# The last row of w4 as a stationary operand, and a result stored from 128 partitions

## Chip, core and metric

One NeuronCore of a Trainium2 chip runs the kernel. The metric is the device time of one execution in microseconds (us); of several runs the median is taken. A separate execution is taken by the hardware profiler. It gives the span from the first to the last instruction, the busy time of each engine and each packet that the 16 DMA engines move.

The engines are PE (TensorE, the matrix unit; the loading of its stationary operand is listed apart as PEld), DVE (VectorE), ACT (ScalarE), POOL (GpSimd) and SP (SyncE, which here only issues transfers).

## The reference

One token `x` of 1024 numbers goes through an attention block over a long cache and, beside it, through a small mixer with an MLP; both results are added to `x`. The batch and the sequence length are 1.

```python
xn = layernorm(x)                              # [1, 1, 1024]
# A: 32 query heads, 4 key/value heads, 65536 cached positions, head size 128
q  = (xn @ wq).reshape(32, 128)                 # wq: [1024, 4096]
p  = softmax(q @ k.T * 128**-0.5)              # k, v: [4, 65536, 128], each for 8 query heads
A  = (p @ v).reshape(4096) @ wo                # wo: [4096, 1024]
# B, with xB = xn
h  = gelu(layernorm(xn) @ w1)                  # w1, w2: [1024, 1024]
hs = shifted(h) @ w2                           # with one position every shift brings in zeros
x1 = xn + hs
B  = x1 + gelu(layernorm(x1) @ w3) @ w4        # w3: [1024, 3584], w4: [3584, 1024]
out = x + A + B
```

All inputs and the output are bf16. Keys and values together are 134 MB and the weights 36 MB, so 170 MB are read for one output of 2 KB.

## The kernel before

**Loads.** SP issues every large load into eight slots of 16 KB per partition. A list `loads` gives their order: wq, w1, w2, w3, then keys and values of eight groups with the four parts of wo between them, and at the end wo's last part and w4. A slot is used again once its last reader is done; SP waits for that ahead of the load, and all loads behind it in the list wait too. w4 has 3584 = 28 x 128 rows, so that each partition holds 28 of them, here called rows 0 to 27. They come as one load of 16 rows (two slots), then rows 16 to 23 in four pieces of two rows, then rows 24 to 27 in pieces of 2, 1 and 1 (`w4_split`). Each piece has a semaphore of its own.

**Layout.** A vector of 1024 numbers has two layouts. In the first, partition p holds the 8 numbers 8p to 8p+7 (`xP`, `xn`, `x1`). In the second, "rows", the numbers lie on 4 partitions (0, 32, 64, 96) with 256 on each. A product of a vector and a matrix is made by `rows_mv` (L440): the vector is the stationary operand, 32 columns wide, of which one column is of use, and the matrix is the moving operand in four parts of 256 columns, one for each quarter of the array (`tile_position`). Its result is in rows, on partitions 0, 32, 64 and 96 of a PSUM bank. Where a product is needed in the first layout, `to_p` (L444) turns it with DVE's 32x32 transpose.

**The sum.** Bank `M1_ps`, columns 0 to 255, gathers in rows what w2 (L440, from `use_w2`), the four parts of wo and all 28 rows of w4 contribute. The rest of the output, x + xn, is kept in rows as `accr`: x is loaded a second time by ACT's queue into `xr_bf` on partitions 0, 32, 64 and 96 (L393, after a memset at L392), and two operations of DVE (L627, L629) normalise it with the sums of the first layer norm and add x. That load shares the semaphore `ch_x` with the load of `xP_bf` (L391), and the cast at L395, from which the first layer norm starts, waits for both.

**The end.** After row 27, DVE adds `accr` and `M1_ps` into `fin`, 128x256 in bf16 of which four partitions are of use (L678), and SP stores these four with one DMA of four pieces of 512 bytes (L679), waits for it and ends.

Each engine runs its own list of instructions in order; `_op` and `_grp` put the waits for semaphores ahead of an instruction by the buffers that it reads and writes (`b_M0`, `b_M1`, `b_fin` and so on). Bank `M0_ps` serves the small products: layer norm sums, the heads' combination and others.

Of the kernel before, what the change touches and what calls it, by code (L numbers as in the profile page):

```python
# [6 lines left out]
BF = mybir.dt.bfloat16  # L7
F32 = mybir.dt.float32
ACTF = mybir.ActivationFunctionType
ALU = mybir.AluOpType  # L10
# [64 lines left out]
def _deps(q, reads, writes):  # L75
    for b in reads:
        for s, v in b.w.items():
            q.wait((s, v))
    for b in writes:
        for s, v in b.w.items():  # L80
            q.wait((s, v))
        for s, v in b.r.items():
            q.wait((s, v))


def _done(ev, reads, writes, partial=False):
    for b in reads:
        b.add_read(ev)
    for b in writes:
        if partial:  # L90
            b.add_write(ev)
        else:
            b.set_write(ev)


def _op(q, fn, reads=(), writes=(), partial=False):
    _deps(q, reads, writes)
    ev = q.op(fn, True)
    _done(ev, reads, writes, partial)
    return ev  # L100


def _grp(q, fns, reads=(), writes=(), partial=False):
    _deps(q, reads, writes)
    ev = None
    for i, fn in enumerate(fns):
        ev = q.op(fn, i == len(fns) - 1)
    _done(ev, reads, writes, partial)
    return ev
# [8 lines left out]
def _dma(q, chan, fn, reads=(), writes=(), partial=False):  # L118
    _deps(q, reads, writes)
    chan.n += 1  # L120
    ev = q.dma(fn, chan.sem, 16 * chan.n)
    _done(ev, reads, writes, partial)
    return ev
# [10 lines left out]
def bass_parallel_sum__gqa_block_cached__mixer_s_mlp__decode_kernel(  # L134
# [14 lines left out]
    P = 128  # L149
    D = A_x.shape[2]  # L150
# [5 lines left out]
    R = D // P  # L156
# [8 lines left out]
    NT = F // P  # L165
    CL = CR // 4
    RW = D // 4
# [7 lines left out]
    with ExitStack() as es:  # L175
# [3 lines left out]
        def sb(name, shape, dt):  # L179
            return E(nc.sbuf_tensor(name, shape, dt))  # L180

        def ps(name, shape, dt):
            return E(nc.psum_tensor(name, shape, dt))

        def sem(name):
            return E(nc.semaphore(name))
# [16 lines left out]
        xP = sb("xP", [P, R], F32)  # L203
        xn = sb("xn", [P, R], F32)
# [6 lines left out]
        ln_s = sb("ln_s", [P, 8], F32)  # L211
# [20 lines left out]
        cb_m = sb("cb_m", [P, 16, R], F32)  # L232
        cb_o = sb("cb_o", [P, R], F32)
        oP_bf = sb("oP_bf", [P, HKV * R + 32], BF)
        xr_bf = sb("xr_bf", [P, RW], BF)
        accr = sb("accr", [P, RW], F32)
        g_bf = sb("g_bf", [P, R + 32], BF)
        ge_x = sb("ge_x", [P, NT], F32)
        ge_a = sb("ge_a", [P, NT], F32)
        ge_b = sb("ge_b", [P, NT], F32)  # L240
        h1g_bf = sb("h1g_bf", [P, R], BF)
        gh_bf = sb("gh_bf", [P, NT + 32], BF)
        fin = sb("fin", [P, RW], BF)

        S_all = ps("S_ps", [P, NCH * 512], F32)
        S_ps = [S_all[:, 512 * i:512 * (i + 1)] for i in range(NCH)]
# [2 lines left out]
        M0_ps = ps("M0_ps", [P, 512], F32)  # L249
        M1_ps = ps("M1_ps", [P, 512], F32)  # L250

        q_pe = _Q("pe", sem("c_pe"))
        q_dve = _Q("dve", sem("c_dve"))
        q_act = _Q("act", sem("c_act"))
        q_pool = _Q("pool", sem("c_pool"))
        q_sp = _Q("sp", None)
        ch_x = _DmaChan(sem("d_x"))
        ch_out = _DmaChan(sem("d_out"))
# [3 lines left out]
        b_ln = _B(); b_qT = _B(); b_Y = _B(); b_misc = _B(); b_ge = _B()  # L262
# [5 lines left out]
        b_Bst = _B(); b_brun = [_B(), _B()]; b_dd = _B(); b_ff = _B()  # L268
        b_p = _B(); b_pT = [_B(), _B()]; b_lcol = [_B(), _B()]; b_lsum = _B(); b_Lacc = _B(); b_O = _B()
        b_cb = _B(); b_oP = [_B() for _ in range(HKV)]  # L270
        b_xr = _B(); b_accr = _B(); b_h1 = _B(); b_gh = _B(); b_fin = _B()


        place = [0]
# [15 lines left out]
        def load(src, width=SLOT):  # L290
            i = take(1, 1)
            view = slots_sb[:, i, 0:width]
            _dma(q_sp, slots[i].chan, lambda e, view=view, src=src: e.dma_start(out=view, in_=src), writes=[slots[i].buf])
            return [(view, [slots[i].buf], i)]
# [94 lines left out]
        b_const.set_write(ev)  # L389

        _dma(q_act, ch_x, lambda e: e.dma_start(out=xP_bf[:, :], in_=A_x[0, 0, :].rearrange("(p r) -> p r", p=P)), writes=[b_xb])  # L391
        _op(q_dve, lambda e: e.memset(xr_bf[:], 0.0), writes=[b_xr])  # L392
        _dma(q_act, ch_x, lambda e: e.dma_start(out=xr_bf[0:P:32, :], in_=A_x[0, 0, :].rearrange("(j m) -> j m", j=4)), writes=[b_xr])  # L393
        b_xb.add_write((ch_x.sem, 16 * ch_x.n))
        _op(q_dve, lambda e: e.tensor_copy(xP[:], xP_bf[:]), reads=[b_xb], writes=[b_x])  # L395

        _op(q_pe, lambda e: e.matmul(M1_ps[:, 0:P], selGT_bf[:, :], selGT_bf[:, :], start=True, stop=True), reads=[b_const], writes=[b_M1])
# [36 lines left out]
        def rows_mv(nkk, parts, st_fn, b_st, b_slot, b_out, first, last, k0=0):  # L434
            fns = []
            for kk in range(k0, k0 + nkk):
                for out_fn, mv_fn in parts:
                    for j in range(4):
                        fns.append(lambda e, kk=kk, j=j, out_fn=out_fn, mv_fn=mv_fn, st=(first and kk == k0), sp=(last and kk == k0 + nkk - 1):
                                   e.matmul(out_fn(j), st_fn(kk), mv_fn(kk, j), start=st, stop=sp, tile_position=(0, 32 * j), skip_group_check=True))  # L440
            _grp(q_pe, fns, reads=b_slot + [b_st], writes=b_out, partial=not first)
# [4 lines left out]
        def gelu(width, dst_bf, b_dst):  # L446
            xs_ = ge_x[:, 0:width]; a_ = ge_a[:, 0:width]; bb_ = ge_b[:, 0:width]
            _op(q_dve, lambda e: e.tensor_copy(xs_, X32[:, 1, 0:32 * width:32]), reads=[b_X[1][0]], writes=[b_ge])
            _op(q_dve, lambda e: e.tensor_tensor(out=a_, in0=xs_, in1=xs_, op=ALU.mult), reads=[b_ge], writes=[b_ge])
            _op(q_dve, lambda e: e.tensor_scalar(out=a_, in0=a_, scalar1=0.044715, scalar2=1.0, op0=ALU.mult, op1=ALU.add), reads=[b_ge], writes=[b_ge])  # L450
            _op(q_dve, lambda e: e.tensor_tensor(out=bb_, in0=a_, in1=xs_, op=ALU.mult), reads=[b_ge], writes=[b_ge])  # L451
            _op(q_act, lambda e: e.activation(a_, bb_, ACTF.Tanh, scale=math.sqrt(2.0 / math.pi)), reads=[b_ge], writes=[b_ge])  # L452
            _op(q_dve, lambda e: e.tensor_scalar(out=a_, in0=a_, scalar1=1.0, scalar2=0.5, op0=ALU.add, op1=ALU.mult), reads=[b_ge], writes=[b_ge])
            _op(q_dve, lambda e: e.tensor_tensor(out=dst_bf, in0=a_, in1=xs_, op=ALU.mult), reads=[b_ge, b_const], writes=[b_dst])
# [23 lines left out]
        def d_parts(view, c0):  # L478
            return [(lambda t: M1_ps[32 * t:32 * t + 32, c0:c0 + RW], lambda kk, t: view[:, kk * D + t * RW:kk * D + (t + 1) * RW])]
# [14 lines left out]
        def use_w3(j, ld):  # L494
# [4 lines left out]
            if j == 3:  # L499
                to_p(S_all[:, 1024:1024 + FW].rearrange("p (c s) -> p s c", s=NT), 0, NT, [b_S[2], b_S[3]])  # L500
                gelu(NT, gh_bf[:, 0:NT], b_gh)

        def use_w4(grp, ld):
            view, parts = ld[0:2]
            for bu, k0, k in parts:
                rows_mv(k, d_parts(view, 0), lambda kk: gh_bf[:, grp * R + kk:grp * R + kk + 32], b_gh, bu, [b_M1],
                        False, grp * R + k0 + k == NT, k0)

        def use_wo(h, ld):
            view, b = ld[0:2]  # L510
# [99 lines left out]
        for g in range(NG):  # L610
# [13 lines left out]
        uses += [("v", NG - 1, a) for a in range(NA)] + [("wo", HKV - 1)] + [("w4", i) for i in range(4)]  # L624

        layer_norm(xP, b_x, xn, xn_bf, b_xn, 0)
        _op(q_dve, lambda e: e.tensor_scalar(out=accr[:], in0=xr_bf[:], scalar1=ln_s[:, 1:2], scalar2=ln_s[:, 4:5], op0=ALU.add, op1=ALU.mult),  # L627
            reads=[b_xr, b_ln], writes=[b_accr])
        _op(q_dve, lambda e: e.tensor_tensor(out=accr[:], in0=accr[:], in1=xr_bf[:], op=ALU.add), reads=[b_xr, b_accr], writes=[b_accr])  # L629
        loaders = {"wq": load_wq, "w1": lambda: load(w1_v[:, 0:SLOT]), "w2": lambda: load(w2_v[:, 0:SLOT]), "w3": load_w3, "wo": load_wo, "w4": load_w4,  # L630
                   "k": load_k, "v": load_v}
        doubles = {"wq", "w3", "k"}
# [42 lines left out]
                taken[i] -= 1  # L675
            issue()
        assert not loads and not ready
        _op(q_dve, lambda e: e.tensor_tensor(out=fin[:], in0=accr[:], in1=M1_ps[:, 0:RW], op=ALU.add), reads=[b_accr, b_M1], writes=[b_fin])  # L678
        ev_out = _dma(q_sp, ch_out, lambda e: e.dma_start(out=out[0, 0, :].rearrange("(j m) -> j m", j=4), in_=fin[0:P:32, :]), reads=[b_fin])  # L679
        q_sp.wait(ev_out)  # L680

        block.sync(lambda e: q_sp.emit(e))
# [32 lines left out]
```

## Time and profile before

| | |
|---|---|
| median of 3 runs | 406.20 us (406.18 to 406.21) |
| the profiled execution's own time | 406.29 us |
| its span, first to last instruction | 404.6 us |
| mean granted TensorE clock | 0.615 |
| busy: PE, PEld, DVE, ACT, POOL | 170.8, 75.4, 200.4, 65.2, 7.5 us |
| bytes moved, mean rate | 170.13 MB, 421 GB/s |
| the largest group of DVE: L522, transposes of keys | 147.7 us, 128 of 1211 ns |

How to read it: a group of instructions is named by line, engine and operation, the tiles that it writes and reads, and its shape; `M_ps` stands for both banks M0 and M1, and `in_B_w_dram` for w1 to w4. An arrow with a name after it tells what ended the idle time before the group. "SPq" and "ACTq" are instructions that issue transfers. A DMA's landing is the moment when its semaphore has its last count. Cut into stages, the page's rows give for each stage the busy time of PE, PEld, DVE, ACT and POOL, the granted clock, the share of time that the 16 DMA engines are busy, and GB/s.

### The profile page before, as it was taken

The page shows a single profiled execution, that of the slowest core. Times are in us where ns is not written, and L with a number is a line of the kernel's source. Part 1 is how long each engine was busy: PE and PEld are TensorE (multiplying, and loading weights), DVE is VectorE, ACT ScalarE, POOL GpSimd, SP SyncE. Part 2 cuts the span into 40 slices and gives each one's busy share as a digit, 9 for nine tenths or more (in the row PEclk, how much of TensorE's full clock was granted, in tenths as well). Part 3 has the DMA queues.
Part 4 walks back from the last instruction along what each step waited for, and adds up shares of the span by engine and source line. Part 5 has one row for each costly group of instructions (what it writes and reads, how often), then busy time and mean ns, then how long its engine had stood idle before and what let it go on. Part 6 is the DMA issues. An engine that isn't in the chain of part 4 may idle for free.

```text
span 404.6 us, 4047 instructions
## 1 busy us (share of the span) xinstructions
PE 170.8 (42%) x1651; PEld 75.4 (19%) x1651; DVE 200.4 (50%) x304; ACT 65.2 (16%) x91; POOL 7.5 (2%) x38
## 2 busy tenths in 40 slices
PE   0273231223555345435335363535252436355626
PEld 0122110102212112211121131212121122122313
DVE  0255027667667665755173737571545655740010
ACT  1000000006007105200610041106010232034000
POOL 5000000000000000000000000000000000000000
PEclk9985655555655965665556655656565657655656
DMA  8999999999999999999999999999999999999995
GB/s 357 421 415 426 452 415 444 413 437 420 462 400 431 429 447 411 441 414 444 411 450 410 437 424 441 415 427 439 423 433 434 423 434 424 420 434 420 444 405 197
DMA packets 9682, 170.13 MB, mean 421 GB/s; under 512 B 1208, under 2 KB 1216, under 8 KB 2112
## 3 DMA queue, kind: packets, MB, share of 16 engines
q1 hardware_dynamic: 9512, 169.88, 98.5%
q8 instruction: 13, 0.21, 0.2%
q14 instruction: 5, 0.04, 0.0%
q10 hardware_dynamic: 152, 0.00, 0.0%
HBM read 169.87 MB, written 0.00 MB: 420 GB/s over the span
## 4 chain that ended last, share of the span: by engine, by line
DMA 57%; DVE 21%; PE 13%; issue 6%; ACT 2%; SPq 0%; POOL 0%; ACTq 0%
DMA slots_sb<-in_A_k_cache_dram 47%; DVE X L522 17%; PE S_ps L529 8%; DMA slots_sb<-in_B_w_dram 7%; DMA xr_bf<-in_A_x_dram 3%; DVE mcol L534 3%; PE OT_ps L575 2%; PE S_ps L440 2%; ACT p_sb L553 1%; ACT pT_sb L565 1%; PE PT_ps L562 1%; PE M_ps L424 0%; PE M_ps L416 0%; PE M_ps L543 0%; SPq L317 0%
## 5 line engine op out<-in xcount | busy, mean ns | idle before, releaser
L522 DVE STREAM_TRANSPOSE X<-slots_sb 128x1024 f32<-128x1024 f32 x128 | 147.7, 1211 | 39.1 <-DMA slots_sb<-in_A_k_cache_dram 39.1
L529 PE MATMUL S_ps<-X,Yall 128*32 128x512 bf16 x512 | 59.9, 614 | 150.4 <-DVE X L522 150.4
L553 ACT ACTIVATE p_sb<-S_ps,brun 128x512 bf16<-128x512 f32 x32 | 45.2, 1412 | 195.5 <-DVE brun L545 105.2
L575 PE MATMUL OT_ps<-slots_sb,pT_sb 128*32 128x512 bf16 x512 | 55.9, 584 | 12.8 <-ACT pT_sb L565 9.6
L534 DVE TENSOR_REDUCE mcol<-S_ps 128x1 f32<-128x512 f32 x32 | 22.1, 692 | 69.2 <-PE S_ps L529 69.2
L529 PEld LDWEIGHTS S_ps<-X,Yall 128*32 128x32 bf16 x512 | 17.3, 126 | 185.8 <-DVE X L522 169.4
L575 PEld LDWEIGHTS OT_ps<-slots_sb,pT_sb 128*32 128x32 bf16 x512 | 18.5, 132 | 37.9 <-issue 32.2
L565 ACT ACTIVATE pT_sb<-PT_ps 128x1024 bf16<-128x1024 bf16 x16 | 16.4, 1023 | 55.6 <-PE PT_ps L562 55.6
L562 PE MATMUL PT_ps<-ident_bf,p_sb 128*128 128x128 bf16 x128 | 15.3, 294 | 11.8 <-ACT pT_sb L565 8.9
L440 PE MATMUL S_ps<-slots_sb,xn_bf 128*32 128x512 bf16 (+1 forms) x128 | 12.6, 567 | 10.7 <-DMA slots_sb<-in_B_w_dram 9.2
L562 PEld LDWEIGHTS PT_ps<-ident_bf,p_sb 128*128 128x128 bf16 x128 | 11.4, 133 | 20.3 <-ACT pT_sb L565 11.0
L592 DVE TENSOR_TENSOR O_acc<-O_acc,OT_ps 128x512 f32<-128x512 f32 x4 | 2.8, 688 | 16.5 <-PE OT_ps L575 16.5
L440 PE MATMUL M_ps<-slots_sb,gh_bf 128*32 128x256 bf16 x112 | 6.5, 399 | 7.7 <-DMA slots_sb<-in_B_w_dram 7.6
L444 DVE STREAM_TRANSPOSE X<-S_ps 128x512 f32<-128x512 f32 (+1 forms) x3 | 2.5, 848 | 14.2 <-PE S_ps L440 14.2
L452 ACT ACTIVATE ge_a<-ge_b 128x8 f32<-128x8 f32 (+1 forms) x2 | 0.4, 217 | 52.2 <-DVE ge_b L451 52.2
L678 DVE TENSOR_TENSOR fin<-accr,M_ps 128x256 bf16<-128x256 f32 x1 | 0.4, 421 | 16.3 <-PE M_ps L440 16.3
L553 ACT ACTIVATION_READ_ACCUMULATOR p_sb<-S_ps,brun 128x1 f32 x32 | 8.5, 264 | 0.0
L440 PE MATMUL M_ps<-slots_sb,oP_bf 128*32 128x256 bf16 x128 | 7.7, 420 | 1.4 <-DVE oP_bf L604 1.4
L597 PE MATMUL M_ps<-O_acc,selX 128*128 128x128 f32 x32 | 8.2, 439 | 0.0
L440 PEld LDWEIGHTS S_ps<-slots_sb,xn_bf 128*32 128x32 bf16 x128 | 4.3, 133 | 17.0 <-DMA slots_sb<-in_B_w_dram 9.9
L597 PEld LDWEIGHTS M_ps<-O_acc,selX 128*128 128x128 f32 x32 | 7.3, 333 | 0.0
L395 DVE CAST xP<-xP_bf 128x8 f32<-128x8 bf16 x1 | 0.2, 172 | 14.2 <-DMA xr_bf<-in_A_x_dram 14.2
(97 smaller groups left out, 70.1 us busy)
## 6 DMA issues: line engine op xcount, KB each, us to landing
slots_sb<-in_A_k_cache_dram SPq DMA_DIRECT2D x16, 4096.0 KB, 26.9
slots_sb<-in_A_v_cache_dram SPq DMA_DIRECT2D x32, 2048.0 KB, 30.7
slots_sb<-in_A_wq_dram SPq DMA_DIRECT2D x2, 4096.0 KB, 16.8
slots_sb<-in_A_wo_dram SPq DMA_DIRECT2D x4, 2048.0 KB, 27.5
slots_sb<-in_B_w_dram SPq DMA_DIRECT2D x2, 3584.0 KB, 33.5
slots_sb<-in_B_w_dram SPq DMA_DIRECT2D x2, 2048.0 KB, 28.1
slots_sb<-in_B_w_dram SPq DMA_DIRECT2D x1, 4096.0 KB, 31.9
slots_sb<-in_B_w_dram SPq DMA_DIRECT2D x5, 512.0 KB, 32.4
```

The costliest lines, as they stand in the source:

```text
L440: e.matmul(out_fn(j), st_fn(kk), mv_fn(kk, j), start=st, stop=sp, tile_position=(0, 32 * j), skip_group_check=True))
L444: _op(q_dve, lambda e: e.transpose(out=X32[:, 1, c0:c0 + 32 * n], in_=src), reads=b_src, writes=[b_X[1][0]], partial=c0 > 0)
L452: _op(q_act, lambda e: e.activation(a_, bb_, ACTF.Tanh, scale=math.sqrt(2.0 / math.pi)), reads=[b_ge], writes=[b_ge])
L522: _op(q_dve, lambda e, ix=ix: e.transpose(out=X32[:, m, 1024 * ix:1024 * (ix + 1)], in_=K32[:, 1024 * ix:1024 * (ix + 1)]), reads=b, write ...
L529: fns.append(lambda e, we=we, c_mid=c_mid, mv=mv: e.matmul(S_ps[ch][32 * c_mid:32 * c_mid + 32, :], Yall[:, h, we, :, :].rearrange("p a g ...
L534: _op(q_dve, lambda e: e.reduce_max(mcol[:, gm, ch:ch + 1], S_ps[ch][:, :], axis=AX.X), reads=[b_S[ch]], writes=[b_mcol[gm]], partial=ch > 0)
L553: _op(q_act, lambda e, ch=ch: e.activation(p_sb[:, :, :, ch], S_ps[ch][:, :].rearrange("p (c i) -> p c i", i=32), ACTF.Exp, bias=brun[:, k ...
L562: _grp(q_pe, [lambda e, i=i, c=8 * c8 + i: e.transpose(out=PT_ps[:, i * P:(i + 1) * P], in_=p_sb[:, c, :, :].rearrange("p i h -> p (i h)") ...
L565: _op(q_act, lambda e, c8=c8, m=m: e.activation(pT_sb[:, m, :, 32 * c8:32 * c8 + 32, :].rearrange("p a x g -> p x a g"), PT_ps[:, :].rearr ...
L575: fns.append(lambda e, cl=cl, q4=q4: e.matmul(OT_ps[32 * q4:32 * q4 + 32, :], pT_sb[:, m, a, 4 * cl:4 * cl + 4, :].rearrange("p x g -> p ( ...
L592: _op(q_dve, lambda e: e.tensor_tensor(out=O_acc[:, :], in0=O_acc[:, :], in1=OT_ps[:, :], op=ALU.add), reads=[b_OT], writes=[b_O])
L597: fns.append(lambda e, t=t: e.matmul(M0_ps[:, 256:384], selX[:, t, :, :].rearrange("p g x -> p (g x)"), O_acc[:, t * P:(t + 1) * P], start ...
```

## The change

The output is gathered in the first layout, on all 128 partitions. `acc` = x + xn is made there with one addition, so the second load of x, its memset and the two operations in rows go. All rows of w4 but the last still go through `rows_mv` into `M1_ps`. When row 26 is done, `turn_acc` turns the sum to 128 partitions with DVE's transpose and adds it to `acc`. Row 27 is multiplied the other way about: for each c of 0 to 7, the 128 columns c, c+8, c+16 and so on of w4's row are the stationary operand (read with a step of 8 elements, 16 bytes), one column of `gh_bf` is the moving operand, and the result is one column of `M0_ps` on 128 partitions. `fin` becomes 128x8, and the store takes 16 bytes from each of 128 partitions.

```diff
-        xr_bf = sb("xr_bf", [P, RW], BF)
-        accr = sb("accr", [P, RW], F32)
+        acc = sb("acc", [P, R], F32)
+        accT = sb("accT", [P, 32 * R], F32)
...
-        fin = sb("fin", [P, RW], BF)
+        fin = sb("fin", [P, R], BF)
...
-        _op(q_dve, lambda e: e.memset(xr_bf[:], 0.0), writes=[b_xr])
-        _dma(q_act, ch_x, lambda e: e.dma_start(out=xr_bf[0:P:32, :], in_=A_x[0, 0, :].rearrange("(j m) -> j m", j=4)), writes=[b_xr])
-        b_xb.add_write((ch_x.sem, 16 * ch_x.n))
...
+        LAST = 1
+
+        def turn_acc():
+            _op(q_dve, lambda e: e.transpose(out=accT[:, :], in_=M1_ps[:, 0:RW].rearrange("p (c r) -> p r c", r=R)), reads=[b_M1], writes=[b_accT])
+            _op(q_dve, lambda e: e.tensor_tensor(out=acc[:], in0=acc[:], in1=accT[:, 0:32 * R:32], op=ALU.add), reads=[b_accT], writes=[b_acc])
+
         def use_w4(grp, ld):
             view, parts = ld[0:2]
             for bu, k0, k in parts:
-                rows_mv(k, d_parts(view, 0), lambda kk: gh_bf[:, grp * R + kk:grp * R + kk + 32], b_gh, bu, [b_M1],
-                        False, grp * R + k0 + k == NT, k0)
+                k1 = grp * R + k0
+                if k1 < NT - LAST:
+                    rows_mv(k, d_parts(view, 0), lambda kk: gh_bf[:, grp * R + kk:grp * R + kk + 32], b_gh, bu, [b_M1], False, k1 + k == NT - LAST, k0)
+                    if k1 + k == NT - LAST:
+                        turn_acc()
+                    continue
+                _grp(q_pe, [lambda e, kk=kk, c=c, st=(k1 == NT - LAST and kk == k0 and c == 0): e.matmul(M0_ps[:, 32 + c:33 + c], view[:, kk * D + c:(kk + 1) * D:R], gh_bf[:, grp * R + kk:grp * R + kk + 1],
+                                                           start=st, stop=(grp * R + kk == NT - 1), skip_group_check=True)
+                            for kk in range(k0, k0 + k) for c in range(R)], reads=bu + [b_gh], writes=[b_M0], partial=k1 > NT - LAST)
...
-        _op(q_dve, lambda e: e.tensor_scalar(out=accr[:], in0=xr_bf[:], scalar1=ln_s[:, 1:2], scalar2=ln_s[:, 4:5], op0=ALU.add, op1=ALU.mult),
-            reads=[b_xr, b_ln], writes=[b_accr])
-        _op(q_dve, lambda e: e.tensor_tensor(out=accr[:], in0=accr[:], in1=xr_bf[:], op=ALU.add), reads=[b_xr, b_accr], writes=[b_accr])
+        _op(q_dve, lambda e: e.tensor_tensor(out=acc[:], in0=xP[:], in1=xn[:], op=ALU.add), reads=[b_x, b_xn], writes=[b_acc])
...
-        _op(q_dve, lambda e: e.tensor_tensor(out=fin[:], in0=accr[:], in1=M1_ps[:, 0:RW], op=ALU.add), reads=[b_accr, b_M1], writes=[b_fin])
-        ev_out = _dma(q_sp, ch_out, lambda e: e.dma_start(out=out[0, 0, :].rearrange("(j m) -> j m", j=4), in_=fin[0:P:32, :]), reads=[b_fin])
+        _op(q_dve, lambda e: e.tensor_tensor(out=fin[:], in0=acc[:], in1=M0_ps[:, 32:32 + R], op=ALU.add), reads=[b_acc, b_M0], writes=[b_fin])
+        ev_out = _dma(q_sp, ch_out, lambda e: e.dma_start(out=out[0, 0, :].rearrange("(p r) -> p r", p=P), in_=fin[:, :]), reads=[b_fin])
         q_sp.wait(ev_out)
```

More of the change, by code (lines that the diff above doesn't have):

```diff
@@ L270, in bass_parallel_sum__gqa_block_cached__mixer_s_mlp__decode_kernel @@
         b_cb = _B(); b_oP = [_B() for _ in range(HKV)]
-        b_xr = _B(); b_accr = _B(); b_h1 = _B(); b_gh = _B(); b_fin = _B()
+        b_acc = _B(); b_accT = _B(); b_h1 = _B(); b_gh = _B(); b_fin = _B()
         place = [0]
```

## The prediction

> **What bounds the kernel now.** I began with the page: is the end set by an engine or by the transfers?
>
> ```profile
> span 404.6 us, 4047 instructions
> ...
> DMA  8999999999999999999999999999999999999995
> ```
>
> The DMA row stands at its highest digit in every slice but the first and the last. DVE, the busiest engine, has 50% of the span. To see whether the digit 9 hides gaps I cut the span into stages:
>
> ```profile
> 20.00:40.00 20.00, 11.49 (x136) 5.85 (x128) 11.14 (x52) 0.21 (x1) 1.10 (x2) 0.70 0.98 418
> 40.00:200.00 160.00, 64.19 (x606) 25.31 (x606) 91.55 (x115) 29.98 (x43) 0.00 (x0) 0.59 1.00 429
> 200.00:380.00 180.00, 80.86 (x736) 35.21 (x740) 92.84 (x119) 33.76 (x47) 0.00 (x0) 0.59 1.01 429
> ...
> 401.70:404.60 2.90, 0.28 (x4) 0.08 (x4) 0.42 (x1) 0.00 (x0) 0.00 (x0) 0.79 0.00 1
> ```
>
> The last two columns are the DMA share and GB/s. From 2.5 to 396 us, the two stages not shown included, the share is 0.98 to 1.01: no wait between engines there lengthens the kernel, for the transfers never pause. The time is therefore the stream of 169.9 MB plus what stands after its last byte. I followed that end in the chain of waits and then in the timeline:
>
> ```profile
> 373.81 27.82 DMA slots_sb<-in_B_w_dram
> 401.64 0.04 issue
> 401.68 0.32 PE M_ps L440 x4
> 402.00 0.02 issue
> 402.03 0.42 DVE fin L678
> ```
>
> ```profile
> 400.54 0.79 PE L440 MATMUL M_ps<-slots_sb,gh_bf 128*32 128x256 bf16 x12 [0.81 <-DMA slots_sb<-in_B_w_dram]
> ...
> 402.48 0.65 SPq L679 DMA_DIRECT2D out_dram<-fin  x1
> ```
>
> After the last piece of w4 lands (401.64) come, one behind the other: four matmuls (0.04 + 0.32), the sum into fin (0.42), the issue of the store (402.48 to 403.13), and its flight: the trace has the four 512-byte packets at 403.72 to 403.78, their semaphores at 404.08 to 404.15, and SP past its wait at 404.17. These 2.5 us are all that an edit of this size can shorten without moving fewer bytes.
>
> **The change part by part, at the start.** It removes a memset, the load of xr_bf on ACT's queue (1.07 us of issue behind that memset, four 512-byte packets) and two DVE operations of 0.41 and 0.42 us at L627 and L629; one 128x8 addition (0.17 us, as L422) takes their place.
>
> ```profile
> 0.79 0.41 ACTq L391 DMA_DIRECT2D xP_bf<-in_A_x_dram  x1
> ...
> 1.24 1.07 ACTq L393 DMA_DIRECT2D xr_bf<-in_A_x_dram  x1
> ...
> 15.27 0.17 DVE L395 CAST xP<-xP_bf 128x8 f32<-128x8 bf16 x1 [14.23 <-DMA xr_bf<-in_A_x_dram]
> ```
>
> Both loads count on one semaphore and L395 waits for both. The trace's landings are 12.82 to 13.15 for xP_bf and 15.12 to 15.25 for xr_bf, so the first layer norm starts 2.1 us sooner, and wq's first half (landed at 12.98) can be used 2.1 us sooner. What is late next is wq's second half, which PE waits for until 22.74 and which the stream sets; from there nothing moves. The load of w3's second half, held on SP until 22.9 by wq's first slots, is issued some 2 us sooner into a queue that already holds 7.5 MB (18 us at 420 GB/s). I cost the whole start at 0; the stream is what hides it. Without that cover it would be worth up to the 2.1 us.
>
> **At the end, PE.** Row 27 of w4 is now 8 loads of 128x128 weights, each with one moving column, where it was 4 loads of 32 columns with 256 moving. No stationary operand in the trace is read with a step of 16 bytes, and none has one moving column in bf16; bounds come from the nearest rows. L468 has four bf16 loads of 128 columns with 32 moving:
>
> ```profile
> 29.20 0.29 PE L468 MATMUL M_ps<-qT_bf,permWE 128*128 128x32 bf16 x4 [1.97 <-DVE qT_bf L467]
> ```
>
> The rows of a transpose and of an addition that the next steps use stand in the views of their lines:
>
> ```profile
> L444 DVE STREAM_TRANSPOSE X<-M_ps x2: 439/444/449, 33.0 to 35.5; 128x256 f32<-128x256 f32 x2
> ...
> L472 DVE TENSOR_TENSOR Yall<-M_ps,maskA x16: 191/191/193, 29.5 to 32.9; 128x32 bf16<-128x32 f32 x16
> ```
>
> A single matmul of L468 takes 0.188, so (0.29 - 0.19) / 3 = 0.034 us from start to start. Eight: 7 x 0.034 + 0.19 = 0.43 against today's 0.32, +0.11. Low end: no longer than today, 0. High end, the f32 loads of L597 (8.2 us for 32, 0.26 each): 7 x 0.26 + 0.44 = 2.26, +1.9. Same type and width decide: +0.11, so fin can start at 402.14.
>
> **The turn.** Row 26's matmuls end at 401.33 (400.54 + 0.79); the 128x256 transpose (0.44, L444, same form from the same bank) and an addition (0.17, L422), each with 0.04 before it, end at 402.02: 0.12 before PE. Cost 0, hidden behind row 27's landing (0.64 after row 26's) and its matmuls. If both rows landed together the turn would end 0.30 + 0.04 + 0.65 + 0.04 behind the landing, some 0.55 later than PE. Behind the turn's wait for PE stands only fin on DVE, and behind fin only the store on SP.
>
> **fin** becomes 128x8 out of PSUM: 0.17 (a copy of that size, L404) to 0.19 (L472, four times as wide), from 0.42: -0.24.
>
> **The store.** One DMA from 128 partitions, 16 bytes each, in place of four of 512. Its issue: the only such shape is xP_bf's at L391, 0.41; full-width loads on SP take 0.33; today's takes 0.65. Between -0.32 and 0 (the issue may go with the queue, not with the shape): -0.24. Flight: today's first packet leaves 0.59 behind the end of the issue, and wq's first, with 128 descriptors, 0.63 behind its own, but its sixteen engines begin over 1.1 us (1.81 to 2.91) at that cold start. Each engine then has 8 packets of 16 bytes instead of one of 512 on four engines. In the load of xP_bf such a packet takes 9 ns and the next small one follows 12 ns on, so 8 take 0.1. Low end 0; high end 1.1 of spread, and 8 full trips to HBM (403.78 to 404.15, 0.37 each, 7 more: 2.6) if they go singly. No row shows a small write; loads of that size pipeline. I take 0.2 of spread and 0.1 of packets: +0.3.
>
> The page DMA: Bandwidth & Descriptors of the Trainium skill (Specifications) wants at least 512 bytes per transfer and says that below it the engine reads, modifies and writes; that speaks against this store. No run here shows a small write to HBM. By the rule each of the 128 pieces would be a read and a write; it is the first rival below.
>
> **Sum.** +0.11 - 0.24 - 0.24 + 0.30 = -0.07 on the profiled execution's own 406.29 us (a span of 404.6 and 1.7 around it): 406.2. The three shown runs have a median of 406.20, 0.09 less, so 406.1 there.
>
> **The rivals.**
>
> 1. The store turns slow, and with it the kernel: an engine's eight 16-byte writes don't overlap. At 0.37 each, 7 x 0.37 = 2.6 where I put 0.1: 408.6. Half overlapped, +1.2: 407.3. It decides from 0.12 us a packet (8 x 0.12 = 0.1 + 0.87, which carries -0.07 past +0.81). For it: the pieces of one engine are neighbours in HBM, four of them in 64 bytes. Against: xP_bf's reads pipeline. 0.20, most likely 407.3.
> 2. The 16-byte step slows the weight load: at L562's pace for half a clock (15.3 us for 128, 0.12 each) 7 x 0.12 + 0.19 = 1.03, 406.7; at L597's, 408.0. Against: L529 reads its moving operand with a step of 4 bytes at no visible price, though that is another port. 0.07, most likely 406.7.
> 3. The earlier start reaches the end: 406.1 - 2.1 = 404.0. For it: 3% of the span's chain is xr_bf's landing. Against: the shares of 0.98 to 1.01 above; a chain names one way back, not the only limit. 0.06.
> 4. The turn isn't hidden, as the change says it is, since the last two pieces land closer: 406.7. 0.03.
>
> **How the numbers follow.** The forecast has 0.64 and, with its smaller unknowns (PE 0 to +0.6, issue -0.32 to 0, flight 0 to +0.8, and 0.2 for how evenly the sixteen engines end), its own range is 405.6 to 406.9. The range for 8 in 10 leaves out the third rival on its lower side and the upper half of the first on its upper side: 405.6 to 407.4. What a measurement of this kernel tells from no change is about 0.2%, 0.81 us, so faster means below 405.4 and slower above 407.0. Faster: rival 3 and 0.06 of the forecast's low end, 0.12. Slower: 0.17 of rival 1, 0.02 of rival 2 and 0.06 of the forecast's high end, 0.25. Within: 0.63.
>
> **What would show it.** In the profile after: L395 starts at about 13.2, wq's last wait still ends at about 22.7, and the DMA share between 40 and 380 us stays at 1.00. The last landing stays near 401.6; if it moves by more than 0.5, the stream was changed, for which these rows give no reason. The eight matmuls should take 0.4 to 0.5, fin under 0.2, the store's issue about 0.4, and from there to SP's end of wait about 1.35 (1.04 today). I am wrong if that last stretch exceeds 2.3, if the matmuls take over a microsecond, or if the end comes some 2 us earlier, for then the first 40 us are not covered by the stream.

## The result, and the profile after

The changed kernel takes 406.89 us (median of 22 runs, 406.62 to 407.19), the kernel before 406.22 beside it (22 runs, 406.15 to 406.45). The ratio is 1.0015, with a 95% interval of 1.0009 to 1.0022: slower, by two thirds of a microsecond. The forecast was 406.1, no change that can be told.

The profiled execution has a span of 405.2 us, 0.69 longer than before. First the place where nothing was to happen, in stages (the last two columns are the DMA share and GB/s):

```profile
20.00:40.00 20.00, 10.70 (x116) 5.48 (x108) 8.98 (x41) 0.21 (x1) 0.70 (x2) 1.00 0.98 419
40.00:200.00 160.00, 67.03 (x606) 26.62 (x606) 91.95 (x117) 29.85 (x43) 0.40 (x1) 0.61 1.00 429
200.00:380.00 180.00, 77.70 (x736) 34.16 (x740) 92.84 (x119) 33.80 (x46) 0.00 (x0) 0.60 1.01 429
```

The stream is the same to within 1 GB/s. The start, from the timeline of the changed kernel:

```profile
13.12 0.17 DVE L392 CAST xP<-xP_bf 128x8 f32<-128x8 bf16 x1 [13.12 <-DMA xP_bf<-in_A_x_dram]
...
20.79 0.33 SPq L302 DMA_DIRECT2D slots_sb<-in_B_w_dram  x1
22.70 0.14 PEld L437 LDWEIGHTS S_ps<-slots_sb,xn_bf 128*32 128x32 bf16 x8 [2.93 <-DMA slots_sb<-in_A_wq_dram]
```

The first cast starts 2.15 us sooner, w3's load is issued 2 us sooner, and PE then stands 2.93 us for wq's second half, until 22.70 as before. Now the end, in the chain of waits:

```profile
373.41 28.20 DMA slots_sb<-in_B_w_dram
401.62 0.05 issue
401.66 0.67 PE M_ps L515 x8
402.33 0.03 issue
402.36 0.02 DVEq L48
402.38 0.04 issue
402.43 0.16 DVE fin L686
```

The last landing is at 401.62 (401.64 before). What follows it differs, and the timeline shows the parts that the chain leaves out:

```profile
401.37 0.45 DVE L503 STREAM_TRANSPOSE accT<-M_ps 128x256 f32<-128x256 f32 x1 [15.53 <-PE M_ps L437]
...
401.85 0.17 DVE L504 TENSOR_TENSOR acc<-acc,accT 128x8 f32<-128x8 f32 x1
...
402.62 0.35 SPq L687 DMA_DIRECT2D out_dram<-fin  x1
```

Last, what SP waited for at its end, first in the kernel before, then in the changed one (total, times, longest, in us):

```profile
SPq L175 <- DMA out_dram<-fin: 1.0, 1, 1.0
```

```profile
SPq L175 <- DMA out_dram<-fin: 1.9, 1, 1.9
```

Put together, from the starts in the trace:

| from the last landing on, us | before | after | difference | forecast |
|---|---|---|---|---|
| last landing | 401.64 | 401.62 | -0.02 | 0 |
| to the start of fin | 0.39 | 0.81 | +0.42 | +0.11 |
| fin, to the issue of the store | 0.45 | 0.19 | -0.26 | -0.24 |
| issue of the store | 0.65 | 0.35 | -0.30 | -0.24 |
| from the issue's end to the end of SP's wait ("flight") | 1.05 | 1.90 | +0.85 | +0.30 |
| sum | | | +0.69 | -0.07 |

Two rows are off. Row 27's matmuls start 0.062 apart where 0.034 was put. The store's 128 packets are all on their way within 0.2 us (403.46 to 403.65), where 0.3 was put for spread and packets together. The store's semaphore gets sixteen counts, one from each engine, here called reports, and some of these are late:

```
semaphore counts of the store, changed kernel:
403.86 403.88 403.89 403.90 403.92 403.93 403.94 403.96 403.97 403.98 | 404.10 404.24 404.38 404.42 404.70 404.85
```

Ten of sixteen engines report in a train, 13 ns apart, 0.2 us behind the last packet; six drop in later, the last 0.86 after the train's end.

### The profile page after: what moved, and what is told of

It reads as the page before. It is cut to its first block, busy times and chain, and to the rows that moved or that the text cites. A ratio compares the mean times of both kernels' runs of the same rounds, so it can differ in the third digit from the quotient of the medians.

```text
span 405.2 us, 4055 instructions
## 1 busy us (share of the span) xinstructions
PE 171.9 (42%) x1655; PEld 76.6 (19%) x1655; DVE 200.1 (49%) x304; ACT 65.1 (16%) x91; POOL 7.5 (2%) x38
## 4 chain that ended last, share of the span: by engine, by line
DMA 59%; DVE 20%; PE 12%; issue 6%; ACT 2%; SPq 0%; ACTq 0%; DVEq 0%
DMA slots_sb<-in_A_k_cache_dram 46%; DVE X L532 17%; PE S_ps L539 7%; DMA slots_sb<-in_B_w_dram 7%; DMA slots_sb<-in_A_wq_dram 5%; DVE mcol L544 3%; PE OT_ps L585 2%; ACT p_sb L563 1%; ACT pT_sb L575 1%; PE S_ps L437 1%; PE PT_ps L572 1%; PE M_ps L553 0%; SPq L317 0%; DVE Rm L551 0%; DVE mrow L550 0%
## 5 line engine op out<-in xcount | busy, mean ns | idle before, releaser
L437 PE MATMUL S_ps<-slots_sb,xn_bf 128*32 128x512 bf16 (+1 forms) x128 | 13.7, 601 | 11.5 <-DMA slots_sb<-in_B_w_dram 8.0
```

## The experiments

Each edit stands against the changed kernel. The kernel before, run beside them, had medians of 406.33 to 406.34; ratios are to it. "Fin at" is the time from the last landing to the start of fin. The last landing itself lies between 401.49 and 401.80 in these profiles, so single profiles are compared by the steps behind it, and kernels by their medians.

**The form of the store.** Theory S said that small pieces meet in the same bytes of HBM; its rival E said that sixteen reports are slower than four.

```diff
-in_=fin[:, :]                 # 128 partitions, 16 bytes
+in_=fin[0:P:8, :]             # e1: fin has 64 columns, 16 partitions, 128 bytes
+in_=fin[0:P:32, :]            # e2: fin has 256 columns, 4 partitions, 512 bytes
```

The diff shows the read of `fin` alone. In these two kernels, and in those with 32 and 64 pieces further down, `fin` is also set to zero at the start and only its first 8 columns are written with sums, so that the output is not the whole result.

> The changed kernel, but the store takes 128 bytes from each of 16 partitions (0, 8, 16 and so on) instead of 16 bytes from each of 128; what is stored is not the sum in its order, only the first 8 of each 64 numbers are sums. In the changed kernel the store's wait ends 1.90 us after the end of its issue (402.96 to 404.86), before the change 1.05. Theory S (the size of the pieces: many small writes that meet in the same few bytes of HBM finish late): one larger piece per engine, the stretch falls to about 1.0 to 1.1, the time to 406.9 - 0.85 = 406.05. Rival E (sixteen engines have to report instead of four, and the slowest of sixteen is late whatever the size): the stretch stays at 1.7 to 1.9, the time at 406.8 to 406.9. Both: issue 0.35, since sixteen engines are used.

Measured: 406.50 (ratio 1.0006, 0.9997 to 1.0015). The flight is 1.20, and all sixteen counts come in one train, 404.15 to 404.35. Rival E falls, although the flight is 0.1 above what theory S put. The issue, though, took 0.59 and not 0.35, a miss of both, which gives back part of the gain:

```profile
402.57 0.59 SPq L688 DMA_DIRECT2D out_dram<-fin  x1
```

> The changed kernel with the store of the kernel before: 512 bytes from each of 4 partitions (the first 8 of each 256 numbers are sums). All that is left of the change at the end is then PE's row 27, the turn and the narrow fin. Both theories S and E: issue back at 0.65, stretch after it back at 1.05, so 0.30 longer and 0.85 shorter than in the changed kernel: 406.9 - 0.55 = 406.35. If instead what was late belongs to the 128-partition matmuls or to a cold store path and not to the store's form, the stretch stays above 1.5 and the time above 406.8.

Measured: 406.44 (1.0002, 0.9993 to 1.0011), issue 0.65, flight 1.03, as said. With the old store the rest of the edit costs 0.1 us by the medians, which the interval doesn't tell from nothing; by the profile the later fin (+0.41) and the narrower one (-0.26) leave +0.15.

**Row 27's weights and fin's waits.**

```diff
-view[:, kk * D + c:(kk + 1) * D:R]
+view[:, kk * D + c * P:kk * D + (c + 1) * P]     # e3
-reads=[b_acc, b_M0], writes=[b_fin]
+reads=[b_M0, b_acc], writes=[b_fin]              # e4
```

With e3's columns row 27's part of the sum lands in another order than the output has, so that kernel is not a complete one.

> The changed kernel, but row 27's weights are 128 neighbouring columns of w4 (step 2 bytes) instead of every eighth (step 16 bytes); the result's order is another. In the changed kernel the eight matmuls start 0.062 us apart, in L468 (neighbouring columns, 32 moving) 0.03. Theory W (the step of 16 bytes slows the weight load): spacing falls to about 0.03, row 27 takes 0.45 instead of 0.66, time 406.9 - 0.2 = 406.7. Rival N (a load of 128 columns behind each matmul of one column costs 0.06 whatever the step): spacing and time stay, 406.9.

Theory W holds in the profile. The first line is row 27 in this kernel, the second in the changed one:

```profile
401.54 0.35 PE L515 MATMUL M_ps<-gh_bf,slots_sb 128*128 128x1 bf16 x8 [0.35 <-DMA slots_sb<-in_B_w_dram]
```

```profile
401.66 0.66 PE L515 MATMUL M_ps<-gh_bf,slots_sb 128*128 128x1 bf16 x8 [0.35 <-DMA slots_sb<-in_B_w_dram]
```

The spacing is 0.025 with neighbouring columns, 0.062 with the step of 16 bytes, and fin is at 0.51 instead of 0.81. What takes longer is the load of the weights itself (shortest, median and longest in ns; neighbouring columns first, then the step):

```profile
L515 PEld LDWEIGHTS M_ps<-gh_bf,slots_sb x8: 95/96/99, 401.5 to 401.7; 128*128 128x128 bf16 x8
```

```profile
L515 PEld LDWEIGHTS M_ps<-gh_bf,slots_sb x8: 140/170/175, 401.7 to 402.1; 128*128 128x128 bf16 x8
```

The clock isn't the reason. It was 1.00 at the start of all eight matmuls with neighbouring columns, and in the repeat of the changed kernel (further down) it was 1.00 through the whole of row 27, whose matmuls again started 0.062 apart. But the time stayed: 406.89 (1.0014, 1.0005 to 1.0022). In the profile SP then waited longer for the store, a flight of 2.44:

```profile
SPq L175 <- DMA out_dram<-fin: 2.4, 1, 2.4
```

> The changed kernel with the two reads of fin named in the other order, so that the wait for PE is the one that fin itself carries and the wait for DVE's own addition stands ahead of it, alone, and is over by 402.0. In the changed kernel the wait for PE is an instruction of its own (402.36) and fin starts 0.07 later (402.43). Theory: fin starts 0.03 to 0.05 after PE's end, 0.05 to 0.07 sooner than now; time 406.9 - 0.06 = 406.83. Rival: the two waits cost the same in any order, time stays at 406.9.

Fin is at 0.73, 0.08 sooner, as the theory has it, and the time is longer, 407.28 (1.0024, 1.0014 to 1.0034), with a flight of 2.17. A miss: two edits that bring fin closer had made nothing faster. In this profile the last landing is also 0.13 later than in the changed kernel's, which adds to its time apart from the store. Either the late reports of the store swallowed the gain, or something held the end to a fixed point; a run below tells these apart.

**Neighbours or smallness.** The same 128 pieces of 16 bytes go to a scratch tensor, at several distances.

```diff
-e.dma_start(out=out[0, 0, :].rearrange("(p r) -> p r", p=P), in_=fin[:, :])
+e.dma_start(out=scr[:, 0:R], in_=fin[:, :])      # scr: 128 rows of 512 (e5), 64 (e6) or 32 bytes (e13)
```

> The changed kernel, but the 128 pieces of 16 bytes go to a scratch tensor in HBM, 512 bytes apart, and the output is left unwritten. Known so far: with 128 bytes from each of 16 partitions the semaphores of all sixteen engines come in one train, 13 ns apart, the stretch from the issue's end to the wait's end is 1.20; with 16 bytes from 128 partitions, neighbours in HBM, it was 1.90, 2.44 and 2.17 in three profiles, ten or eight engines report in such a train and the others drop in over another 0.9 to 1.4 us. Theory L (pieces that lie in the same stretch of HBM wait for one another): far apart they land together, stretch 1.1 to 1.3, time 406.9 - 0.7 = 406.2. Rival N (a 16-byte write is slow wherever it goes, and eight per engine add up): stretch stays at 1.8 to 2.4, time 406.8 to 407.

> As the kernel with pieces 512 bytes apart, but 64 bytes apart, the output again left unwritten. Theory L with a stretch of HBM of 64 bytes or less: as fast as 512 apart, stretch 1.1 to 1.3, time about 406.2. Theory L with a longer stretch than 64 bytes: in between, 1.4 to 1.9, 406.4 to 406.8. Rival N: as slow as neighbours, 1.8 to 2.4, 406.8 to 407.

512 apart: 406.15 (0.9996, 0.9987 to 1.0005), flight 1.11. 64 apart: 406.11 (0.9995, 0.9987 to 1.0004), flight 1.11, all counts in one train. SP's wait in the kernel with 64 bytes:

```profile
SPq L175 <- DMA scr<-fin: 1.1, 1, 1.1
```

So a write of 16 bytes isn't slow by itself, and 128 of them don't add up: rival N falls, theory L holds, with a unit of 64 bytes or less. One thing differs besides the distance: these pieces go to another tensor. No run writes neighbours into the scratch tensor. Against the tensor as the cause speak the stores of larger pieces into the output, of which none is late, and the first of the two stores of 16-byte pieces further down.

> The changed kernel, but the store takes 64 bytes from each of 32 partitions (0, 4, 8 and so on; the first 8 of each 32 numbers are sums). Two pieces per engine, neighbours, each a full 64 bytes. Theory L with 64 bytes or less, and also rival N in the form that only pieces under 64 bytes are slow: stretch 1.1 to 1.3. Theory L with a longer stretch of HBM: 1.4 to 1.9. Issue: 0.35 with 128 partitions, 0.59 with 16 and 0.65 with 4, so 0.5 to 0.6 here; time 406.3 to 406.5, or 406.6 to 407 by the longer stretch.

406.46 (1.0003, 0.9994 to 1.0012), issue 0.55, flight 1.20, as said.

> The changed kernel itself once more, to stand beside the others on the same chip. If the late landings of the small pieces vary from one execution to the next, its stretch differs from the 1.90 of its first profile while all steps up to the issue's end stay within 0.05 of theirs (row 27's matmuls 0.062 apart, fin 0.81 behind the last landing); the time 406.7 to 407.2. If they are fixed, the stretch is again 1.9.

406.98 (1.0016, 1.0007 to 1.0025). Fin is again at 0.81, and the flight is 1.86. Eight engines report in the train, eight later, the last 0.85 behind it. So in these two executions the number of late engines changes, and the last one's delay hardly; in the profiles of the two edits above the last report came 1.4 and 1.2 behind the train.

**Is the end held to a fixed point?**

```diff
-e.dma_start(out=out[0, 0, :].rearrange("(p r) -> p r", p=P), in_=fin[:, :])
+e.dma_start(out=scr[:, 0:R], in_=fin[:, :])
-view[:, kk * D + c:(kk + 1) * D:R]
+view[:, kk * D + c * P:kk * D + (c + 1) * P]
-reads=[b_acc, b_M0], writes=[b_fin]
+reads=[b_M0, b_acc], writes=[b_fin]
```

> Pieces 64 bytes apart in a scratch tensor (the output left unwritten), and in it both edits that brought nothing by themselves: neighbouring columns as row 27's weights and fin's two waits in the other order. In their own profiles they brought fin 0.30 and 0.08 closer to the last landing (0.51 and 0.73 where the changed kernel has 0.81), but the flight of the store was longer by as much or more. Theory: these steps are on the path and their gain was lost in the scatter of the store's late pieces; with a store whose pieces land together (stretch 1.11) it shows: fin 0.43 to 0.47 behind the last landing, time 406.11 - 0.35 = 405.75. Rival: something else holds the end to a fixed point, so that whatever comes sooner waits longer: time stays at 406.1.

405.82 (0.9987, 0.9978 to 0.9996), 0.29 less than with 64 bytes apart alone. Its timeline:

```profile
401.57 0.35 PE L516 MATMUL M_ps<-gh_bf,slots_sb 128*128 128x1 bf16 x8 [0.35 <-DMA slots_sb<-in_B_w_dram]
...
402.03 0.16 DVE L687 TENSOR_TENSOR fin<-acc,M_ps 128x8 bf16<-128x8 f32 x1
402.22 0.33 SPq L688 DMA_DIRECT2D scr<-fin  x1
```

Fin is at 0.51, where 0.43 to 0.47 was put, the flight is 1.11, and nothing holds the end. The gain of row 27 is real, and with the store's neighbouring pieces it was lost in their late reports. The other order of fin's waits adds nothing here: the turn's addition now ends at 401.92, together with PE.

**What must not be shared.**

> The changed kernel, but the store takes 32 bytes from each of 64 partitions (the first 8 of each 16 numbers are sums): two pieces share 64 bytes of HBM instead of four. Theory: pieces that share 64 bytes wait for one another, some 0.14 a step; with two of them there are fewer steps: stretch 1.25 to 1.6, issue 0.35 to 0.55, time 406.4 to 406.7. Rival: the shared unit is 32 bytes, then no piece is late, stretch 1.1 to 1.2, time 406.2 to 406.4.

406.57 (1.0006, 0.9998 to 1.0015), issue 0.56, flight 1.22, one train:

```profile
SPq L175 <- DMA out_dram<-fin: 1.2, 1, 1.2
```

The time lies in the theory's range and above the rival's 406.2 to 406.4, and the flight at the upper edge of the rival's. The issue accounts for that: it takes 0.2 more than with 128 partitions. What decides is the train: no engine is late, and the flight is that of the stores with 16 and 32 pieces (1.20). So the rival holds: two pieces of 32 bytes in the same 64 don't disturb each other.

> The changed kernel, but the store writes only 256 bytes, 16 bytes from each of 16 partitions, neighbours in HBM, the rest of the output left unwritten: one piece for each engine, and each 64 bytes are shared by four engines. Theory X (pieces of different engines that share 64 bytes wait for one another): some engines report late, stretch 1.3 to 1.8. Rival O (only pieces that follow one another on the same engine do): all report in one train, stretch 1.1 to 1.25. Issue 0.5 to 0.6 as with other stores from 16 partitions.

406.49 (1.0004, 0.9995 to 1.0013), issue 0.58, flight 1.19, one train, as rival O put it: with sixteen pieces, one for each of the sixteen engines that report, none is late although two share 32 bytes. A delay of one engine within the train of 0.2 us would not show, however, and the run has fewer pieces as well, so it doesn't by itself show that only pieces of the same engine disturb each other.

> The changed kernel, but the 128 pieces of 16 bytes go to a scratch tensor, 32 bytes apart, the output left unwritten. Theory 32 (a piece waits for another in the same 32 bytes): each piece has its 32 bytes alone, so all land in one train, stretch 1.11, time 406.1 as with 64 bytes apart. Rival 64 (sharing 64 bytes is enough for pieces smaller than that unit): some engines late, stretch 1.4 to 1.9, time 406.4 to 406.8.

406.12 (0.9995, 0.9986 to 1.0004), flight 1.12, one train:

```profile
SPq L175 <- DMA scr<-fin: 1.1, 1, 1.1
```

So among the distances tried, 128 pieces of 16 bytes are late 16 bytes apart and not late 32 apart: they may share 64 bytes but not 32.

**The store in two, by partition.**

```diff
-ch_out = _DmaChan(sem("d_out"))
+ch_out = _DmaChan(sem("d_out")); ch_odd = _DmaChan(sem("d_odd"))
...
-ev_out = _dma(q_sp, ch_out, lambda e: e.dma_start(out=out[0, 0, :].rearrange("(p r) -> p r", p=P), in_=fin[:, :]), reads=[b_fin])
+ev_out = _dma(q_sp, ch_out, lambda e: e.dma_start(out=out[0, 0, :].rearrange("(p t r) -> t p r", t=2, r=R)[0], in_=fin[0:P:2, :]), reads=[b_fin])
+ev_odd = _dma(q_act, ch_odd, lambda e: e.dma_start(out=out[0, 0, :].rearrange("(p t r) -> t p r", t=2, r=R)[1], in_=fin[1:P:2, :]), reads=[b_fin])
 q_sp.wait(ev_out)
+q_sp.wait(ev_odd)
```

> The changed kernel with the store in two: even partitions on SP, odd ones on ACT's queue, so that within a store every piece of 16 bytes has its 32 bytes alone and its neighbour is in the other store, at about the same time. Issue 0.56 on both queues at once, as with 64 partitions before. Theory 32 with waiting only inside one store's own run of pieces: stretch 1.15 to 1.3, time 406.4 to 406.6. Rival (any two pieces in flight in the same 32 bytes wait for one another): stretch 1.6 to 2.2, time 406.9 to 407.3.

407.70 (1.0032, 1.0019 to 1.0044), and a flight of 2.50. It went the rival's way and beyond what the rival put (1.6 to 2.2, 406.9 to 407.3). Both issues took 0.55 to 0.56 side by side, SP's packets left from 403.78 on and ACT's 0.27 behind them:

```profile
SPq L48 <- DMA out_dram<-fin: 2.5, 1, 2.5
```

```
SP's store:  404.14 ... 404.33 (fifteen in a train) 404.70
ACT's store: 404.42 404.44 404.45 404.47 404.84 404.86 405.02 405.17 405.25 405.26 405.27 405.41 405.58 405.59 405.60 405.62
```

Within each store every piece has its 32 bytes alone. The first store has fifteen of its sixteen reports in a train, although its pieces are 16 bytes long and go to the output. The second came while the first was being written, and its reports spread over 1.20 us where a train takes 0.20. If shared bytes are the reason, the delay isn't confined to pieces that follow one another on one queue. But no run has two stores at once that share nothing, so it isn't shown that a second store on ACT's queue would otherwise be on time.

**The start.**

In the kernel with pieces 64 bytes apart (the lines that only declare `xr_bf` left out):

```diff
+_op(q_dve, lambda e: e.memset(xr_bf[:], 0.0), writes=[b_xr])
+_dma(q_act, ch_x, lambda e: e.dma_start(out=xr_bf[0:P:32, :], in_=A_x[0, 0, :].rearrange("(j m) -> j m", j=4)), writes=[b_xr])
+b_xb.add_write((ch_x.sem, 16 * ch_x.n))
```

> Pieces 64 bytes apart (the output left unwritten), with the second load of x, its memset and its wait put back at the start, its data unused. The cast at the start goes back from 13.1 to about 15.2. Theory (the start is covered by the stream of loads): the last landing stays at 401.5 to 401.7 and the time at 406.1. Rival (the 2.1 us reach the end): 408.2; in part, anything above 406.4.

406.18 (0.9998, 0.9989 to 1.0007), 0.07 more than without, which is inside the scatter of both. The cast is back at 15.3 and the last landing at 401.56:

```profile
15.32 0.17 DVE L397 CAST xP<-xP_bf 128x8 f32<-128x8 bf16 x1 [14.28 <-DMA xr_bf<-in_A_x_dram]
```

The store's forms side by side:

| pieces, bytes | issue, us | flight, us | median, us |
|---|---|---|---|
| 4 of 512 | 0.65 | 1.03 | 406.44 |
| 16 of 16, neighbours (256 bytes in all) | 0.58 | 1.19 | 406.49 |
| 16 of 128 | 0.59 | 1.20 | 406.50 |
| 32 of 64 | 0.55 | 1.20 | 406.46 |
| 64 of 32 | 0.56 | 1.22 | 406.57 |
| 128 of 16, neighbours, the changed kernel twice | 0.35 | 1.90, 1.86 | 406.89, 406.98 |
| the same with e3's and with e4's edit | 0.35 | 2.44, 2.17 | 406.89, 407.28 |
| 64 and 64 of 16, on two queues | 0.55, 0.56 | 2.50 | 407.70 |
| 128 of 16, 32, 64 or 512 apart (scratch) | 0.33 | 1.12, 1.11, 1.11 | 406.12, 406.11, 406.15 |

## Why the prediction was right or wrong, point by point

**Right.** What bounds the kernel (the stream, whose last landing moved by 0.02); the start at 0, shown both by the trace and by putting the load back; the turn hidden behind row 27, ending at 402.02 as worked out; fin at -0.24 (-0.26); the store's issue at -0.24 (-0.30); the 0.3 for the packets' spread and their own time, of which they took 0.2. The last landing ends a stretch in which the transfers run dry (before the change the DMA share is 0.57 from 398 to 400 us and 0.22 from 400 to 401.7); the prediction counts it with the stream, and this edit leaves it as it is.

**Wrong, the store's flight.** The step reads "I take 0.2 of spread and 0.1 of packets: +0.3". It measured +0.85 and is 0.55 of the 0.76 by which the sum failed. Spread and packets were no more than that, 0.2 together. The value taken gave nothing to late reports of pieces that lie side by side; alone in their 32 bytes the same pieces fly 1.11 to 1.12, +0.06. That the distance makes them late is measured; that pieces in the same 32 bytes wait for one another is the reading that fits all runs but needs one condition more, since sixteen such pieces on sixteen engines weren't late. I took the load of xP_bf for the nearest row and read it wrongly: the 12 ns there lie between the last 16-byte packet of an engine and the 4-byte count behind it (12.555 and 12.567). The sixteen engines' 16-byte packets before that come in rounds some 1.2 us apart (3.63, 4.95, 6.17 and so on), while wq is loaded beside them. So the row shows that such a packet is short (9 ns), not that eight of them follow closely, and it says nothing on writes to HBM that share bytes. The first rival had the place and, in part, the sign: it priced a chain of full trips, 0.37 each, decisive from 0.12 a packet. But its mechanism was that an engine's eight small writes don't overlap, which the pieces 32 bytes and more apart refute, and that the pieces are neighbours was mentioned only as a point in its favour.

The page DMA: Bandwidth & Descriptors of the Trainium skill (Specifications) gives 512 bytes as the least for full rate and reading and rewriting below that. A store of this size doesn't measure a rate; in its latency, pieces of 16 bytes alone in their 32 were as quick as four of 512 (1.11 against 1.05). Here the measurement decides: lying 16 bytes apart, not staying under 512 bytes, made the store late.

**Wrong, row 27.** The step reads "Same type and width decide: +0.11". It measured +0.36 for the matmuls themselves (0.66 instead of 0.29), and 0.06 more until fin. The step of 16 bytes makes 0.30 of it: 0.062 apart against 0.025. The second rival named it and priced it too high, at 0.12. The 0.06 is a wait of its own for PE, which stands ahead of fin since fin waits for two semaphores; the sum had no term for it. With the two waits in the other order fin starts 0.04 behind PE's end instead of 0.11.

The page TensorE: Matmul & The Clock Gate of the Trainium skill (Weight-path perf modes) lists the fast load of 128 weights for packed and strided columns alike. The traces have the weights read as four chunks of 32 with the step and with neighbouring columns alike, and with the step the spacing is still two and a half times as long (0.062 against 0.025).

**The result as a whole.** +0.42 - 0.26 - 0.30 + 0.85 - 0.02 = +0.69 by the profiles, +0.67 by the medians. The 406.89 lie inside the stated range of 405.6 to 407.4, but that is in part luck: the upper part of the range was there for writes that don't overlap, which isn't what happened. With row 27 at the spacing that I put (0.034; 0.025 with neighbouring columns) and pieces that don't meet, the edit would be near the 405.82 measured with both, where fin is 0.11 later than before the change and the flight 0.06 longer. That kernel leaves the output unwritten, though: 128 pieces of 16 bytes fill a vector of 2 KB side by side, and neighbouring columns in a matmul put neighbouring numbers on different partitions. No complete kernel tried here beats the one before.

**Open.** Why the kernel with the other order of waits came out 0.3 slower than the changed kernel itself, with all its steps from the last landing to the issue as fast or faster: its late pieces were later (flight 2.17), for which no run shows a reason, nor for the 2.44 with neighbouring columns. Why one 16-byte piece per engine isn't late although neighbours share 32 bytes; the traces don't tell which engine writes which piece, and the same 128 pieces in another order weren't tried. And whether the second of two stores is late by the shared bytes or by being the second.

## What to carry to other kernels

Price a store by what its pieces share at the destination, not only by their number and size: here 128 pieces of 16 bytes flew 1.1 us as long as each had 32 bytes to itself, and 1.9 us side by side, while pieces of 32 bytes side by side weren't late. Where a small result can lie on few partitions in long pieces, what a narrower operation and a shorter issue win (0.56 us here) is easily lost in the store (0.85 us). And read a stationary operand with neighbouring columns where its load is on the path (0.10 us for a load instead of 0.17).

## What the runs showed of the hardware that wasn't expected

The issue of a store on SP is shortest with 128 partitions, 0.33 to 0.35 us, and takes 0.55 to 0.65 with 64 to 4, though sixteen engines are used in all but the last. The reports of sixteen engines arrive 13 ns apart, so that the train alone takes 0.2 us. A second store, from another queue and into the other halves of the 32-byte units of one just under way, spread its reports over 1.2 us; that the shared units are the reason isn't shown.
